# Short blocks from the last to the first, on one side of each matmul of the first phase

## The chip, the cores and the metric

The kernel runs on one core of one Trainium2 chip. The metric is the device time of one execution in microseconds (us); the time of a kernel is the median of several executions. The core has TensorE (PE in the profile; PEld is its loading of weights), VectorE (DVE), ScalarE (ACT), GpSimd (POOL) and SyncE (SP), which issues nearly all of the DMAs.

## The reference

An attention without softmax, normed, feeds a feed-forward block with softplus:

```python
kv  = np.einsum('bhsd,bhse->bhde', k, v)          # (8, 8, 64, 64)
out = np.einsum('bhsd,bhde->bhse', q, kv)         # (8, 8, 576, 64)
rms = np.sqrt(np.mean(out * out, axis=-1, keepdims=True) + 1e-06)
x   = (out / rms * g_norm) -> (4608, 512)
h   = x @ w_in                                    # (4608, 2048)
g   = np.maximum(h, 0.0) + np.log1p(np.exp(-np.abs(h)))
return g @ w_out                                  # (4608, 512)
```

Nearly all of the work is in the last two products.

## The kernel before, in words

**Three factors for each product.** TensorE takes its operands as fp32r. To keep more of the fp32 digits, every operand is split into three pieces (ACT makes the first, DVE the second and third), and every product of two operands is a sum of three matmuls, piece by piece.

**Phases.** The kernel goes through the tokens three times. The *first phase* handles 12 blocks of NT = 384 tokens. In it the attention of the block is computed too (L696 the keys with the values, L720 the rows), the weights are converted and split, and the first chunks of 128 hidden columns are worked off: four chunks each in blocks 0 to 3, six in blocks 4 to 11 (FIRST). That makes 64 steps of one block and one chunk. The later phases (`wide_step`, 48 steps of 512 tokens) take the remaining chunks and add up the partial results.

**A step of the first phase** (`step`) is:

- `mm1` (L864): 12 matmuls of 128x128 weights on a streamed operand of 384 columns, three pieces times four parts of d_model. All 12 accumulate in one PSUM bank `h` (two banks take turns). The weights are pieces of w_in, the streamed operand pieces of x.
- ACT reads `h` and writes the softplus to SBUF as `g` (L886), then makes the first piece `gv[0]` from `g` (L888). DVE makes the second and third piece (L875, L879).
- `mm2` (L871): three times three matmuls. The weights are 128-column parts of `gv`, the streamed operand is a piece of w_out with 512 columns, and the result accumulates over all chunks of the block in one of three banks (`mine`, s0 to s2).
- After the last chunk of a block, `leave` copies each of the three banks to SBUF on ACT (L931) and stores it.

**Order of the work.** The order of the instructions of each engine is made by a planner at build time (`Plan.order`): every task has a cost in ns, a due position and the slots of memory that it takes and gives back, and the planner plays the program through. It has a step's mm2 due one and a half steps after its mm1, so on TensorE mm1 of one step and mm2 of the step before alternate; the small attention matmuls go between them. A change of a task's contents that leaves its cost and slots alone doesn't change the order.

**Traversal of an operand.** `from_the_end(x, w)` cuts the columns of x into blocks of w and goes through the blocks from the last to the first, and through the columns of a block in natural order; w = 0 leaves x as it is. Where the streamed operand and the result of a matmul are both given so, each column of the result stays at its place. Before the change it is used three times: in mm1, for the last of the 12 matmuls alone, with w = 1 on both sides; in `product` (L1066, the first product of the wide steps, 256 columns) with w = 16 and 8 in turn on both sides; and in the wide `mm2` (L1137, 512 columns) with w = 128 on both sides. All other matmuls are in natural order on both sides.

Of the kernel before, what the change touches and what calls it, by code (L numbers as in the profile page):

```python
# [12 lines left out]
AF = mybir.ActivationFunctionType  # L13
# [5 lines left out]
P = 128  # L19
# [4 lines left out]
E = 1.0 / RADIX  # L24
# [17 lines left out]
def from_the_end(x, w):  # L42

    return x.rearrange("p (b w) -> p b w", w=w)[:, ::-1] if w else x


class Slot:
# [13 lines left out]
class Plan:  # L61
# [19 lines left out]
    def slot(self, ring):  # L81
        return Slot(ring)

    def add(self, engine, ns, run, after=(), pos=0.0, take=(), give=(), size=0, behind=None, follows=None, kind="all"):
        pos, behind = round(pos, 4), None if behind is None else round(behind, 4)
        t = Task(engine, ns, run, [a for a in after if a is not None], pos, list(take), list(give), size)
        for s in t.give:
            s.readers += 1
        self.tasks.append(t)
        t.follows = follows  # L90
        t.behind = behind
        t.kind = kind
        return t
# [113 lines left out]
def kernel(  # L207
# [24 lines left out]
    nc = tc.nc  # L232
    B, H, S, D = q.shape
    d_model, d_ff = moe_w_in.shape
# [3 lines left out]
    KD, KF = d_model // P, d_ff // P  # L238
    NT = 384
    TB = NT // P  # L240
# [12 lines left out]
    LAST = 2  # L253
# [32 lines left out]
    scale = const.tile([P, 1], F32, name="scale")  # L286
# [21 lines left out]
    for i in range(3):  # L308
# [10 lines left out]
                 h=2, o=2, tp=1, s0=1, s1=1, s2=1, s3=1, w=15, wh=3, u=4, u1=1, gvp=2, xl=2, ab=2)  # L319
# [9 lines left out]
    slot, add = plan.slot, plan.add  # L329
# [519 lines left out]
    def step(s):  # L849
        n, c = ORDER[s]  # L850
        cs = CHUNKS[n]
        h, g, gv = slot("h"), slot("g"), slot("gv")
        if c == cs[0]:
            sums[:] = [slot(f"s{i}") for i in range(TB)]
        xv, w_in, w_out = xv_slots[n], w_slots[0, c], w_slots[1, c]
        mine = list(sums)
        kept = c >= 4

        def mm1():
            hp = new(h, [P, NT])  # L860
            for m in range(3 * KD):
                i, kd = divmod(m, KD)
                w = 1 if m == 3 * KD - 1 else 0
                nc.tensor.matmul(from_the_end(hp, w), lhsT=w_in.tile[:, i, kd * P:(kd + 1) * P], rhs=from_the_end(xv.tile[:, i, kd], w),  # L864
                                 start=(m == 0), stop=(m == 3 * KD - 1))

        def mm2(i):
            if c == cs[0]:
                new(mine[i], [P, d_model])
            for m in range(3):  # L870
                nc.tensor.matmul(mine[i].tile, lhsT=gv.tile[:, m, i * P:(i + 1) * P], rhs=w_out.tile[:, m],  # L871
                                 start=(c == cs[0] and m == 0), stop=(c == cs[-1] and m == 2))

        def low():
            nc.vector.tensor_tensor(out=gv.tile[:, 1], in0=g.tile, in1=gv.tile.bitcast(F32)[:, 0], op=ALU.subtract)  # L875

        def less():
            f32 = gv.tile.bitcast(F32)
            nc.vector.scalar_tensor_tensor(out=gv.tile[:, 2], in0=f32[:, 1], scalar=-RADIX, in1=f32[:, 0],  # L879
                                           op0=ALU.mult, op1=ALU.add)  # L880

        a = add("PE", 2100, mm1, x_split[n] + factors_done[0, c] + [m for _, m in mm1s[-1:]] +
                (factors_done[1, ORDER[s - 2][1]] if s > 1 else []), s, [h],
                ([xv] if c == cs[-1] else []) + ([w_in] if s == last_step[c] and c != 4 else []))
        mm1s.append((s, a))
        a = add("ACT", 490, lambda: nc.scalar.activation(new(g, [P, NT]), h.tile, func=AF.Softplus, scale=1.0 + E),  # L886
                [a], s, [g], [h])
        a = add("ACT", 530, lambda: nc.scalar.activation(new(gv, [P, 3, NT], F32R)[:, 0], g.tile, func=AF.Copy, scale=DOWN),  # L888
                [a], s, [gv])
        a = add("DVE", 570, low, [a], s, [], [g])  # L890
        a = add("DVE", 570, less, [a], s)
        for i in range(TB):
            a2 = add("PE", 700, lambda i=i: mm2(i), [a] + factors_done[1, c] + [mm2s.get(i)], s + 1.5,
                     [mine[i]] if c == cs[0] else [],
                     [gv] + ([w_out] if s == last_step[c] and not kept else []))
            mm2s[i] = a2
            if c == cs[-1]:
                leave(0, n * TB + i, mine[i], a2, s + 1.5)
# [14 lines left out]
    def leave(ph, t, bank, done, pos):  # L913

        ot = slot("m")
        if ph == LAST and t == n_tiles - 1:
            mid = d_model // 2
            dst = out[t * P:(t + 1) * P]

            def left():  # L920
                nc.scalar.activation(new(ot, [P, d_model])[:, :mid], bank.tile[:, :mid], func=AF.Copy, scale=scale)

            def right():
                nc.vector.tensor_scalar(out=ot.tile[:, mid:], in0=bank.tile[:, mid:], scalar1=scale, scalar2=None, op0=ALU.mult)

            a = add("ACT", 390, left, [done] + scale_done, pos, [ot], [bank])
            b = add("DVE", 430, right, [done] + scale_done, pos + 0.01, [], [bank], follows=a)
            add("SP", 350, lambda: nc.sync.dma_start(out=dst[:, :mid], in_=ot.tile[:, :mid]), [a], pos, [], [ot], 400)
            add("ACT", 100, lambda: nc.scalar.dma_start(out=dst[:, mid:], in_=ot.tile[:, mid:]), [b], pos, [], [ot], 400)
            return  # L930
        a = add("ACT", 690 if ph == LAST else 600, lambda: nc.scalar.activation(  # L931
            new(ot, [P, d_model]), bank.tile, func=AF.Copy, scale=scale if ph == LAST else 1.0),
            [done] + (scale_done if ph == LAST else []), pos, [ot], [bank])
        if ph == LAST and BY_PE <= t < n_tiles - TB:
            n, i = divmod(t, TB)

            def store():
                for m in range(P // BL):
                    a, u = divmod(P // BL * i + m, TB)
                    row = n * NT + u * P + a * BL  # L940
                    nc.sync.dma_start(out=out[row:row + BL], in_=ot.tile[m * BL:(m + 1) * BL])

            add("SP", 1600, store, [a], pos, [], [ot], 750)
            return
        dst = out[t * P:(t + 1) * P] if ph == LAST else dram.tile([P, d_model], F32, name=f"part{ph}_{t}")
        st = add("SP", 350, lambda: nc.sync.dma_start(out=dst, in_=ot.tile), [a], pos, [], [ot], 720)
        part.setdefault(t, []).append((dst, st))
# [96 lines left out]
    def wide_step(k):  # L1044
# [14 lines left out]
        def product(u, q):  # L1059
            f, i = PRODUCTS[u]  # L1060
            w = forms[p][f].tile
            dst, v = unit_slots[ph, n, u]
            for m in range(3):
                for kd in range(2):
                    at = i * 2 * P + kd * P
                    nc.tensor.matmul(from_the_end(place(q), (16, 8)[kd]), lhsT=w[:, m, at:at + P],  # L1066
                                     rhs=from_the_end(dst.tile[:, m, v, kd] if u < 6 else dst.tile[:, m, kd], (16, 8)[kd]),
                                     start=(u == 0 and not m and not kd), stop=(m == 2 and kd == 1), skip_group_check=True)
# [92 lines left out]
        for c in range(2):  # L1161
            for i in range(TW):
                slot_pos = b + PACE + MM2[TW * c + i]
                a2 = add("PE", 700, lambda c=c, i=i: mm2(c, i),
                         [split_done[c]] + factors_done[1, 2 * p + c] + ([seeds[i]] if i in seeds and not c else []) +
                         ([before[i]] if c or not first else []), slot_pos, [mine[i]] if first and not c and ph < LAST else [], [gv] + ([outs[c]] if final else []))
                before[i] = a2
                if last and c:
                    leave(ph, TW * n + i, mine[i], a2, slot_pos)
# [45 lines left out]
    for s in range(len(ORDER)):  # L1215
        step(s)
# [51 lines left out]
```

## Time and profile before

| | |
|---|---|
| three runs | 858.67, 860.09 and 861.0 us; median 860.09 |
| the profiled execution | 858.61 us; span 856.8 us |
| granted TensorE clock | 1.0 of full speed |
| PE, DVE, ACT busy, share of the span | 98%, 82%, 61% |
| L864 (mm1 of the first phase) | 768 matmuls of 384 columns |
| L871 (mm2 of the first phase) | 576 matmuls of 512 columns |
| L1066 and L1137 (wide steps) | 2016 of 256 columns, 1152 of 512 columns |
| L886 softplus, 128x384 | 64, 491 ns each |
| L931 copy of a bank, 128x512 | 72 without scale, 595 ns each |

The first phase takes up the span to about 358 us. Matmuls run in a pipeline: the duration that the profile gives to one (334 to 390 ns) holds its way through the array, and the next one starts before it ends. So the durations of matmuls don't add up to time; the distance from start to start does. In the chain of work that ended last, each piece is given with its start and the time until the next piece takes over, so there the sums over a group of matmuls are that distance times their number.

### The profile page before, as it was taken

Reading aid. Unit: us, or ns where it says so; the run is one execution under the profiler, and the core shown is the slowest. Engines: PE = TensorE matmul, PEld = TensorE weight load, DVE = VectorE, ACT = ScalarE, POOL = GpSimd, SP = SyncE. Lnnn points to the kernel's source line nnn. Section 1 sums busy time; section 2 is a strip of 40 time slices with the busy share of each in tenths; the row PEclk is TensorE's granted clock in tenths of the full one; section 3 lists DMA queues with packets and bytes.
Section 4 is the critical chain, followed back from the end, with each engine's and each line's share of the span. In section 5 each row is a group of like instructions: output and inputs, shape, how many; then the busy total and the mean of one; then the engine's idle time right before and its main releaser. Section 6 shows DMA issues by size and latency. Waiting matters only on the chain.

```text
span 856.8 us, 17075 instructions
## 1 busy us (share of the span) xinstructions
PE 843.8 (98%) x6464; PEld 754.7 (88%) x6464; DVE 704.1 (82%) x995; ACT 520.2 (61%) x980; POOL 76.1 (9%) x79
## 2 busy tenths in 40 slices
PE   7899999999999999999999999999999999999998
PEld 5678898999898999998999999998999899999996
DVE  7988898888788889798898788878788766788873
ACT  6866665446344567776667665655868555566654
POOL 0342224111113300000000000000000000000000
PEclk9999999999999999999999999999999999999999
DMA  9998997778784755436645456645354753777864
GB/s 275 301 228 218 264 270 244 178 243 221 215 186 118 194 159 183 143 112 202 211 156 167 160 160 203 197 158 182 124 195 138 234 167 103 241 242 239 250 189 130
DMA packets 239778, 167.07 MB, mean 195 GB/s; under 512 B 106320, under 2 KB 198736, under 8 KB 239696
## 3 DMA queue, kind: packets, MB, share of 16 engines
q1 hardware_dynamic: 239392, 165.86, 65.8%
q8 instruction: 50, 0.82, 0.4%
q14 instruction: 32, 0.26, 0.1%
q10 hardware_dynamic: 304, 0.13, 0.1%
HBM read 112.98 MB, written 52.95 MB: 194 GB/s over the span
## 4 chain that ended last, share of the span: by engine, by line
PE 94%; DVE 2%; ACT 1%; DMA 1%; issue 1%; POOL 1%; SPq 0%; DVEq 0%; ACTq 0%
PE banks L1137 31%; PE banks L1066 28%; PE banks L871 16%; PE banks L864 15%; PE banks L720 2%; PE banks L696 2%; DMA loads<-in_v_dram 1%; DMA raw<-in_moe_w_in_dram 0%; PE banks L738 0%; POOL roots L728 0%; PE banks L1232 0%; DVE half L732 0%; DVE m L464 0%; DVE m L460 0%; DVE units L643 0%
## 5 line engine op out<-in xcount | busy, mean ns | idle before, releaser
L1137 PE MATMUL banks<-pieces,gv 128*128 128x512 f32 x768 | 236.8, 390 | 0.0
L1137 PE MATMUL banks<-pieces,g_False 128*128 128x512 f32 x384 | 149.4, 389 | 0.0
L1137 PEld LDWEIGHTS banks<-pieces,gv 128*128 128x128 f32 x768 | 132.5, 188 | 17.2 <-DVE banks L910 0.2
L864 PE MATMUL banks<-units,pieces 128*128 128x384 f32 x768 | 145.6, 338 | 0.0
L871 PE MATMUL banks<-pieces,gv 128*128 128x512 f32 x576 | 143.3, 393 | 0.0
L864 PEld LDWEIGHTS banks<-units,pieces 128*128 128x128 f32 x768 | 135.5, 188 | 4.5
L871 PEld LDWEIGHTS banks<-pieces,gv 128*128 128x128 f32 x576 | 106.2, 188 | 19.0
L1066 PEld LDWEIGHTS banks<-units,pieces 128*128 128x128 f32 x840 | 111.0, 188 | 6.5 <-ACT banks L1112 0.4
L1066 PE MATMUL banks<-units,pieces 128*128 128x256 f32 x840 | 115.2, 280 | 0.0
L886 ACT ACTIVATE half<-banks 128x384 f32<-128x384 f32 x64 | 31.4, 491 | 95.7 <-PE banks L864 89.8
L1127 DVE TENSOR_TENSOR gv<-g_True,gv 128x1024 fp32r<-128x1024 f32 x47 | 57.5, 1223 | 36.3 <-ACT gv L1124 36.3
L1137 PEld LDWEIGHTS banks<-pieces,g_False 128*128 128x128 f32 x384 | 72.1, 188 | 15.0
L1066 PEld LDWEIGHTS banks<-units,w 128*128 128x128 f32 x504 | 66.7, 188 | 3.7 <-ACT banks L1112 0.2
L1066 PE MATMUL banks<-units,w 128*128 128x256 f32 x504 | 69.6, 280 | 0.0
L728 POOL TENSOR_TENSOR roots<-roots,half 128x8 f32<-128x8 f32 x36 | 61.9, 1720 | 3.0
L1130 DVE SCALAR_TENSOR_TENSOR g_False<-gv 128x1024 fp32r<-128x1024 f32 x47 | 57.6, 1225 | 1.5
L1029 DVE TENSOR_TENSOR units<-loads,units 128x1024 fp32r<-128x1024 f32 x42 | 51.2, 1219 | 6.0 <-ACT units L1026 5.9
L1094 ACT ACTIVATE g_True<-banks 128x256 f32<-128x256 f32 x96 | 36.7, 384 | 30.6 <-PE banks L1066 29.9
L1116 DVE TENSOR_TENSOR g_True<-banks,g_True 128x512 f32<-128x512 f32 x48 | 33.1, 690 | 25.8 <-PE banks L1066 19.8
L931 ACT ACTIVATE m<-banks 128x512 f32<-128x512 f32 x72 | 42.1, 595 | 17.7 <-PE banks L1137 12.5
L1032 DVE SCALAR_TENSOR_TENSOR units<-units 128x1024 fp32r<-128x1024 f32 x42 | 51.4, 1224 | 1.7
L1026 ACT ACTIVATE units<-loads 128x1024 fp32r<-128x1024 f32 x42 | 44.4, 1056 | 12.7 <-PE banks L1066 10.1
(115 smaller groups left out, 1248.5 us busy)
## 6 DMA issues: line engine op xcount, KB each, us to landing
loads<-x SPq DMA_DIRECT2D x180, 128.0 KB, 2.7
part<-m SPq DMA_DIRECT2D x72, 256.0 KB, 2.9
m<-part SPq DMA_DIRECT2D x72, 256.0 KB, 3.5
loads<-form SPq DMA_DIRECT2D x45, 256.0 KB, 3.2
form<-loads SPq DMA_DIRECT2D x36, 256.0 KB, 3.0
raw<-in_moe_w_in_dram SPq DMA_DIRECT2D x16, 512.0 KB, 4.6
loads<-in_k_dram SPq DMA_DIRECT2D x32, 256.0 KB, 4.5
loads<-in_v_dram SPq DMA_DIRECT2D x32, 256.0 KB, 4.6
```

The costliest lines, as they stand in the source:

```text
L728: nc.gpsimd.tensor_tensor(out=r.tile, in0=r.tile, in1=half, op=ALU.pow)
L864: nc.tensor.matmul(from_the_end(hp, w), lhsT=w_in.tile[:, i, kd * P:(kd + 1) * P], rhs=from_the_end(xv.tile[:, i, kd], w), start=(m == 0), ...
L871: nc.tensor.matmul(mine[i].tile, lhsT=gv.tile[:, m, i * P:(i + 1) * P], rhs=w_out.tile[:, m], start=(c == cs[0] and m == 0), stop=(c == cs ...
L931: a = add("ACT", 690 if ph == LAST else 600, lambda: nc.scalar.activation(new(ot, [P, d_model]), bank.tile, func=AF.Copy, scale=scale if p ...
L1026: nc.scalar.activation(part_of(0, F32R), xl.tile if m > 1 else xl.tile[:, 0], func=AF.Copy, scale=DOWN)
L1029: nc.vector.tensor_tensor(out=part_of(1, F32R), in0=xl.tile if m > 1 else xl.tile[:, 0], in1=part_of(0), op=ALU.subtract)
L1032: nc.vector.scalar_tensor_tensor(out=part_of(2, F32R), in0=part_of(1), scalar=-RADIX, in1=part_of(0), op0=ALU.mult, op1=ALU.add)
L1066: nc.tensor.matmul(from_the_end(place(q), (16, 8)[kd]), lhsT=w[:, m, at:at + P], rhs=from_the_end(dst.tile[:, m, v, kd] if u < 6 else dst. ...
L1094: nc.scalar.activation(dst, src, func=AF.Softplus, scale=1.0 + E)
L1127: nc.vector.tensor_tensor(out=gvt(1, F32R), in0=gt(), in1=gvt(0), op=ALU.subtract)
L1130: nc.vector.scalar_tensor_tensor(out=gt(F32R), in0=gvt(1), scalar=-RADIX, in1=gvt(0), op0=ALU.mult, op1=ALU.add)
L1137: nc.tensor.matmul(from_the_end(mine[i].tile, P), lhsT=(gvt(m, F32R) if m < 2 else gt(F32R))[:, c, i * P:(i + 1) * P], rhs=from_the_end(ou ...
```

## The change

In blocks 1 to 10 of the first phase, one side of every matmul of mm1 is taken in short blocks from the last to the first: either the streamed operand (SHORT[n][0]) or the result (SHORT[n][1]). The other side stays in natural order, so the columns of `h` stand in another order than the tokens; ACT's softplus takes that back, by reading `h` or writing `g` in the same blocks. In mm2 it is the same with LONG: the streamed columns of w_out or the columns of the result. Here the copy in `leave` takes the order back. Block by block, the two products have opposite sides, and the length of the blocks is 16, 16, 1, 1, 8, 8, 4, 4, 32, 32 for blocks 1 to 10. Blocks 0 and 11 are natural throughout, and the reversed last matmul of mm1 is gone in all blocks. The wide steps and the planner's costs are as before.

```diff
+SHORT = [(0, 0), (16, 0), (0, 16), (1, 0), (0, 1), (8, 0), (0, 8), (4, 0), (0, 4), (32, 0), (0, 32), (0, 0)]
+LONG = [(0, 0), (0, 16), (16, 0), (0, 1), (1, 0), (0, 8), (8, 0), (0, 4), (4, 0), (0, 32), (32, 0), (0, 0)]
...
             for m in range(3 * KD):
                 i, kd = divmod(m, KD)
-                w = 1 if m == 3 * KD - 1 else 0
-                nc.tensor.matmul(from_the_end(hp, w), lhsT=w_in.tile[:, i, kd * P:(kd + 1) * P], rhs=from_the_end(xv.tile[:, i, kd], w),
+                nc.tensor.matmul(from_the_end(hp, SHORT[n][1]), lhsT=w_in.tile[:, i, kd * P:(kd + 1) * P],
+                                 rhs=from_the_end(xv.tile[:, i, kd], SHORT[n][0]),
                                  start=(m == 0), stop=(m == 3 * KD - 1))
...
             for m in range(3):
-                nc.tensor.matmul(mine[i].tile, lhsT=gv.tile[:, m, i * P:(i + 1) * P], rhs=w_out.tile[:, m],
+                nc.tensor.matmul(from_the_end(mine[i].tile, LONG[n][1]), lhsT=gv.tile[:, m, i * P:(i + 1) * P],
+                                 rhs=from_the_end(w_out.tile[:, m], LONG[n][0]),
                                  start=(c == cs[0] and m == 0), stop=(c == cs[-1] and m == 2))
...
-        a = add("ACT", 490, lambda: nc.scalar.activation(new(g, [P, NT]), h.tile, func=AF.Softplus, scale=1.0 + E),
+        a = add("ACT", 490, lambda: nc.scalar.activation(from_the_end(new(g, [P, NT]), SHORT[n][0]), from_the_end(h.tile, SHORT[n][1]),
+                                                         func=AF.Softplus, scale=1.0 + E),
                 [a], s, [g], [h])
...
+        r, w = LONG[t // TB] if ph == 0 else (0, 0)
         a = add("ACT", 690 if ph == LAST else 600, lambda: nc.scalar.activation(
-            new(ot, [P, d_model]), bank.tile, func=AF.Copy, scale=scale if ph == LAST else 1.0),
+            from_the_end(new(ot, [P, d_model]), r), from_the_end(bank.tile, w), func=AF.Copy, scale=scale if ph == LAST else 1.0),
             [done] + (scale_done if ph == LAST else []), pos, [ot], [bank])
```

## The prediction

> **What bounds the kernel now.** I read the page's busy times first, then its chain of work that ended last.
>
> ```profile
> PE 843.8 (98%) x6464; PEld 754.7 (88%) x6464; DVE 704.1 (82%) x995; ACT 520.2 (61%) x980; POOL 76.1 (9%) x79
> ...
> PE 94%; DVE 2%; ACT 1%; DMA 1%; issue 1%; POOL 1%; SPq 0%; DVEq 0%; ACTq 0%
> PE banks L1137 31%; PE banks L1066 28%; PE banks L871 16%; PE banks L864 15%; PE banks L720 2%; PE banks L696 2%; DMA loads<-in_v_dram 1%; DMA raw<-in_moe_w_in_dram 0%; PE banks L738 0%; POOL roots L728 0%; PE banks L1232 0%; DVE half L732 0%; DVE m L464 0%; DVE m L460 0%; DVE units L643 0%
> ```
>
> TensorE is the bound: 94% of the chain is PE, and the two lines that the change edits (L864, the first product, and L871, the second) are 31% of it. So what counts is the time from one matmul's start to the next, its pitch. The chain in order of time gives pitches as sums (start us, us, line, matmuls). Here is a stretch of the first phase:
>
> ```profile
> 185.00 0.07 PE banks L696 x3
> 185.06 2.29 PE banks L871 x9
> 187.36 2.08 PE banks L864 x12
> 189.44 2.04 PE banks L871 x9
> 191.49 2.11 PE banks L864 x12
> ```
>
> Three things are to be seen. (a) Settled, a 384-column matmul takes 2.08 / 12 = 173.3 ns and a 512-column one 2.04 / 9 = 226.7 ns. The difference, 53.3 ns for 128 columns, is 0.417 ns a column; so 160.0 + 13.3 and 213.3 + 13.3: each matmul has 13.3 ns on top. (b) A first product that follows a settled second product takes 2.11, not 2.08: by the starts in the trace its first matmuls are 171, 175, 178, 185, 176, 182 ns apart, then 173.3. I call this unsettled; it costs 26 ns. After an unsettled second product the next first product is settled (2.08). (c) A second product after other work is unsettled too (2.29): starts 341, 240, 235, 233, 236, 224, 231, 236, 228 apart; without the first gap, in which its weights are loaded, that is 45 to 50 ns over eight times 226.7. But straight after a first product it is settled (2.04). The last of a first product's twelve matmuls is the only one in this phase with both sides reversed, column by column.
>
> The same view where the two phases meet, and one line from the whole span's chain:
>
> ```profile
> 341.70 0.71 PE banks L1066 x6
> 342.42 2.08 PE banks L864 x12
> 344.50 4.08 PE banks L871 x18
> 348.58 2.11 PE banks L864 x12
> ```
>
> ```profile
> 469.92 2.80 PE banks L1066 x24
> ```
>
> L1066 streams 256 columns with both sides in blocks of 16 and 8 from the end. After it L864 is settled (2.08); after natural L871 it is not (2.11). L1066 after natural order is itself unsettled (0.71 for six against 2.80 / 4 = 0.70). So in these rows what calms a group is the order of the matmul **before** it. And 2.80 / 24 = 116.7 ns is 106.7 for 256 columns by (a) plus 10.0: 3.3 ns less than the 13.3 of natural order.
>
> **The change, part by part.** Blocks 0 to 3 have four steps each and blocks 4 to 11 six. Blocks 1 to 10 change: 54 steps, so 54 x 12 = 648 first-product and 54 x 9 = 486 second-product matmuls. Odd blocks (26 steps) stream the first product's operand in short blocks and write the second's result so; even blocks (28) the other way round. Blocks 0 and 11 lose the reversed last matmul. No instruction, wait or DMA is added or moved, and the planner's costs (490, 600) stay as they are, so the order on every queue is the same. Only durations can change.
>
> *PE, settled pitch.* One reversed side alone is not in the trace. Both sides reversed are: blocks of 128 (L1137) and natural order both give 226.7; single columns cost nothing (a 2.08 group holds one; at double time it would take 2.24); blocks of 16 and 8 go with 3.3 ns less, at 256 columns only. So the ends for a matmul are -3.3 ns and, if it never settles, the mean of the unsettled rows: 177.8 - 173.3 = +4.4 in the first product and 49 / 8 = +6 in the second. I take 0, the row at these widths, where single columns and blocks of 128 gave 0. Ends: -3.3 x 1134 = -3.8 us; +4.4 x 648 + 6 x 486 - 1.2 (unsettled already) = +4.6 us.
>
> *PE, unsettled starts.* Of the 54 first products in blocks 1 to 10, 45 are unsettled now: 45 x 26 ns = 1.2 us. I take it that a reversed side calms the group after it, and that only one of the two sides has this effect; which, I don't know. Either way one parity of blocks keeps today's picture (an effective first product, a natural second one), and in the other it turns round: the first product is calmed (-26 ns), and the second follows an uncalmed first product (+45 ns). About 40 of the 54 second products follow directly; the rest are unsettled already. With 28 steps: 28 x 40/54 x 45 = +0.93, less 28 x 45/54 x 26 = -0.61: +0.3 us (26 steps give the same). Blocks 0 and 11 lose the calming end before some four directly following groups: 4 x 45 = +0.2 us. Ends: -1.8 us if all settle (1.2, and 12 interrupted second products x 50 ns), and +40 x 45 = +1.8 us if nothing calms.
>
> *ACT.* The softplus (54) and the copy out of the bank (30) take the order back, on one side each.
>
> ```profile
> L931 ACT ACTIVATE m<-banks 128x512 f32<-128x512 f32 x72 | 42.1, 595 | 17.7 <-PE banks L1137 12.5 <-PE banks L871 2.6 <-DVE m L464 1.2
> ...
> L886 ACT ACTIVATE half<-banks 128x384 f32<-128x384 f32 x64 | 31.4, 491 | 95.7 <-PE banks L864 89.8 <-DVE w L751 3.1 <-DVE units L643 2.7
> ```
>
> No ACT row reads or writes short blocks. The nearest are a square that reads 128-column blocks (L793, 597 ns, as L931) and, on DVE, a transpose that writes 32-element blocks 96 apart (L819, 707 ns against L751's 687). I take +0 ns, the ACT row; the ends are 0 and double (982 and 1190 ns). What hides it is the wait of PE's order, seen in the timeline:
>
> ```profile
> 174.44 2.20 PE L871 MATMUL banks<-pieces,gv 128*128 128x512 f32 x9
> 174.63 0.49 ACT L886 ACTIVATE half<-banks 128x384 f32<-128x384 f32 x1 [3.10 <-PE banks L864]
> 175.16 0.52 ACT L888 ACTIVATE gv<-half 128x384 fp32r<-128x384 f32 x1
> ...
> 175.71 0.56 DVE L875 TENSOR_TENSOR gv<-half,gv 128x384 fp32r<-128x384 f32 x1 [1.73 <-ACT gv L888]
> ...
> 176.38 0.56 DVE L879 SCALAR_TENSOR_TENSOR gv<-gv 128x384 fp32r<-128x384 f32 x1
> ```
>
> The piece that L879 finishes at 176.94 is first used by the second product at 178.58: 1.64 us of cover, more than the 0.49 of a doubled softplus. This is the usual value; in the changed blocks six steps have under 1 us, and two under 0.5 (steps 7 and 48). The bank that a copy frees is written again 2.4 us after the copy's end at the least in nearly all blocks. Were ACT's price doubled, 54 x 0.49 + 30 x 0.6 = 44 us would be added to an engine that is busy 119 of the 226 us from 110 to 336, and some three uncovered steps would cost 0.5 us each: +1.5 us. DVE reads the softplus's output in natural order as before: 0.
>
> *Sum:* 0 + 0.3 + 0.2 + 0 = **+0.5 us**. The profiled execution took 858.61 us (span 856.8 and 1.8 around it), so 859.1 by it. The median of the three runs is 860.09, 1.5 above: I forecast 860.6.
>
> **The rivals.** *Faster: short blocks take 3.3 ns off whichever side has them, and all groups settle.* -3.8 - 1.1 (most of the 1.8) = -4.9 us: 855.2. For it: L1066's 10.0 against 13.3. Against: the reversed matmuls at 384 and 512 columns show no gain, both of L1066's sides are reversed, and at 397.37 the chain has 24 of the same instructions in 2.95 us, so the 10.0 isn't the pattern's alone. If only the streamed side gains (26 x 12 + 28 x 9 = 564 matmuls), -1.9 + 0.5 = -1.4 us: no change.
>
> *Slower: with one side reversed the pitch never settles.* Every matmul pays the unsettled mean: +4.6 us, 864.7, and with the doubled ACT 866.2. It decides from 2.6 / 1134 = 2.3 ns a matmul. For it: L1066 has stretches at 120 and 121, 122, 116, 118 ns for 18 matmuls on end after a break, so the unsettled state can last. Against: every natural group here is settled after nine matmuls at most, and both patterns are natural on one side.
>
> *Slower: single columns in the result cost the bank's write a second pass.* Those are 72 first-product matmuls (block 4) and 36 second-product ones (block 3): at double streaming time 72 x 160 + 36 x 213 = +19.2 us; with the +0.5, 879.8. Against: the last matmul of every first product writes so, in a 2.08 group. The Trainium skill speaks for it: "PSUM — Partial Sum Buffer", Specifications, says that any non-contiguous pattern slows matmuls significantly. By that rule, the trace doesn't agree: L1066's 116.7 and L1137's 226.7 are written in reversed blocks at no cost.
>
> **How the numbers follow.** No change (within 0.3%, about what a measurement of this kernel can tell) is likeliest: 0.52, with 860.6 and its own range 857.6 to 862.6. Faster 0.16. Slower 0.32: 0.22 for the pitch that doesn't settle, 0.06 for an ACT price above double that uncovers the steps, 0.04 for single columns. The range goes from 855.2 (the first rival) to 866.2 (the second with the ACT price); beyond it lie single columns, most of ACT above double, and a gain larger than L1066's.
>
> **What would show it.** Sums of L864 and L871 in the chain, block by block: 2.08 or 2.11 and 2.04 or 2.09 as forecast; 2.04 and 2.01 in the fast rival; over 2.13 and 2.09 in all blocks in the slow one. Blocks 3 and 4 alone far above 2.2 would be single columns. L886 and L931's means show ACT's price, and idle time of PE before L871 whether it is uncovered. I am wrong at the root if one reversed side does something that neither both nor none did, for which the trace has no row.

## The result and the profile after

| | before | after |
|---|---|---|
| median | 859.53 us (8 runs) | 861.73 us (8 runs) |
| ratio, 95% interval | 1 | 1.0029 [1.0016, 1.0041] |
| the profiled execution, its span | 858.61, 856.8 us | 863.54, 861.7 us |
| start of the first mm1 in the span | 43.75 us | 46.47 us |
| first phase, start of the first mm1 to start of the last mm2 | 313.67 us | 315.86 us |

The ratio is worth 2.5 us (1.4 to 3.5 by its interval); the medians are 2.2 us apart. The two profiled executions are 4.9 us apart: 2.7 of it lies ahead of the first changed instruction (in the profiles below that start wanders between 43.5 and 46.5, whatever the kernel; the granted clock of the first 43 us was 1.00 in the profile before and 0.96 in the one after), 2.2 in the first phase and nothing behind it. So the first phase by the trace, 2.2 us, is the change's price, and it is the measure used below, since it has little noise: in the two kernels below that leave the first phase as it was ("wide_natural" and "wide_sides") it is 313.69 us against 313.67 before.

The page after, its busy times and its chain:

```profile
PE 846.0 (98%) x6464; PEld 755.4 (88%) x6464; DVE 704.2 (82%) x995; ACT 520.3 (60%) x980; POOL 76.4 (9%) x79
...
PE banks L1144 30%; PE banks L1073 27%; PE banks L875 16%; PE banks L867 15%; PE banks L724 2%; PE banks L700 2%; DMA loads<-in_k_dram 1%; PE banks L742 0%; POOL roots L732 0%; PE banks L780 0%; DVE half L736 0%; PE banks L1239 0%; DVE roots L728 0%; DVE units L647 0%; ACT w L806 0%
```

TensorE is the bound as before (L867 is now mm1, L875 mm2, L1073 and L1144 the wide steps), and ACT's time is the same. Here is the chain in order of time (start us, us, line, matmuls): the last mm1 of block 4 (result in single columns) and its last two mm2 (165.47 and 169.68, streamed operand in single columns), then mm1 and mm2 of block 5 (streamed operand of mm1 and result of mm2 in blocks of 8):

```profile
163.38 2.08 PE banks L867 x12
165.47 2.10 PE banks L875 x9
167.57 2.10 PE banks L867 x12
169.68 2.10 PE banks L875 x9
171.78 2.11 PE banks L867 x12
173.88 2.04 PE banks L875 x9
175.93 2.15 PE banks L867 x12
178.08 2.05 PE banks L875 x9
```

Where the result is reversed, the sums are those of natural order: 2.04 to 2.09 for nine and, over all of these groups that follow an mm2 directly, mostly 2.08 to 2.11 for twelve. Where the streamed operand is, mm2 takes 2.10, and by the starts all the way through the group: 233.3 ns a matmul, 20 ns on top of the columns where natural order settles at 13.3. For a streamed mm1 the price isn't one number: in block 5 it takes 2.10 and 2.11 in the first two steps and 2.15 in the others, there with 180 ns from the third matmul on. Two more rows answer to those shown of before, the copy and the softplus on ACT:

```profile
L938 ACT ACTIVATE m<-banks 128x512 f32<-128x512 f32 x72 | 42.1, 595 | 18.6 <-PE banks L1144 12.5 <-PE banks L875 2.7 <-DVE m L468 1.8
...
L891 ACT ACTIVATE half<-banks 128x384 f32<-128x384 f32 x64 | 31.5, 492 | 98.7 <-PE banks L867 95.8 <-DVE units L647 2.9
```

595 and 492 ns against 595 and 491: putting the order back is free on ACT here, in every block (487.8 to 493.3 ns in the mean of each of blocks 1 to 10, single columns included).

Added up over all pairs of neighbouring matmuls of mm1 and mm2 (breaks for other work left out), the time above 173.3 and 226.7 ns a matmul is 1.96 us in the first phase before and 4.13 after, a difference of 2.17 us: the whole of the change's price. By part, against before, with the same groups of the first experiment beside it ("natural", which loses the reversed end of mm1 and has no short blocks):

| groups | after, us | natural, us | short blocks alone |
|---|---|---|---|
| mm2 of even blocks (after: streamed in short blocks) | +1.36 | +0.80 | +0.56 |
| mm1 of odd blocks (after: streamed in short blocks) | +0.61 | +0.03 | +0.58 |
| mm2 of odd blocks (after: result reversed, behind a streamed mm1) | +0.32 | +0.72 | -0.40 |
| mm1 of even blocks (after: result reversed, behind a streamed mm2) | -0.26 | -0.06 | -0.20 |
| blocks 0 and 11 (natural order in both) | +0.14 | +0.11 | +0.03 |

So the price has three parts: the lost reversed end of mm1 (1.6 us of the 2.2, the column "natural"), the groups that stream short blocks (+0.56 and +0.58), and what these give back by calming the group behind them (-0.40 and -0.20).

### The profile page after: what moved, and what is told of

The parts are those of the page before. It is cut to its first block, busy times and chain, and to the rows that moved or that the text cites. A ratio compares the mean times of both kernels' runs of the same rounds, so it can differ in the third digit from the quotient of the medians.

```text
span 861.7 us, 17075 instructions
## 1 busy us (share of the span) xinstructions
PE 846.0 (98%) x6464; PEld 755.4 (88%) x6464; DVE 704.2 (82%) x995; ACT 520.3 (60%) x980; POOL 76.4 (9%) x79
## 4 chain that ended last, share of the span: by engine, by line
PE 94%; DVE 2%; DMA 1%; ACT 1%; POOL 1%; issue 0%; SPq 0%; POOLq 0%; DVEq 0%; ACTq 0%
PE banks L1144 30%; PE banks L1073 27%; PE banks L875 16%; PE banks L867 15%; PE banks L724 2%; PE banks L700 2%; DMA loads<-in_k_dram 1%; PE banks L742 0%; POOL roots L732 0%; PE banks L780 0%; DVE half L736 0%; PE banks L1239 0%; DVE roots L728 0%; DVE units L647 0%; ACT w L806 0%
## 5 line engine op out<-in xcount | busy, mean ns | idle before, releaser
L1144 PE MATMUL banks<-pieces,gv 128*128 128x512 f32 x768 | 236.8, 390 | 0.0
L1144 PE MATMUL banks<-pieces,g_False 128*128 128x512 f32 x384 | 149.4, 389 | 0.0
L1144 PEld LDWEIGHTS banks<-pieces,gv 128*128 128x128 f32 x768 | 132.4, 188 | 17.1 <-DVE banks L916 0.2
L867 PE MATMUL banks<-units,pieces 128*128 128x384 f32 x768 | 145.8, 339 | 0.0
L875 PE MATMUL banks<-pieces,gv 128*128 128x512 f32 x576 | 145.2, 397 | 0.0
L867 PEld LDWEIGHTS banks<-units,pieces 128*128 128x128 f32 x768 | 135.7, 188 | 4.8
L875 PEld LDWEIGHTS banks<-pieces,gv 128*128 128x128 f32 x576 | 106.2, 188 | 20.5
L1073 PEld LDWEIGHTS banks<-units,pieces 128*128 128x128 f32 x840 | 111.0, 188 | 6.4 <-ACT banks L1119 0.4
L1073 PE MATMUL banks<-units,pieces 128*128 128x256 f32 x840 | 115.2, 280 | 0.0
L1144 PEld LDWEIGHTS banks<-pieces,g_False 128*128 128x128 f32 x384 | 72.1, 188 | 15.1
L1073 PEld LDWEIGHTS banks<-units,w 128*128 128x128 f32 x504 | 66.7, 188 | 3.7 <-ACT banks L1119 0.2
L1073 PE MATMUL banks<-units,w 128*128 128x256 f32 x504 | 69.6, 280 | 0.0
L880 DVE TENSOR_TENSOR gv<-half,gv 128x384 fp32r<-128x384 f32 x64 | 35.4, 554 | 21.0 <-ACT gv L894 20.8
```

What stands on the lines that cost most here:

```text
L867: nc.tensor.matmul(from_the_end(hp, SHORT[n][1]), lhsT=w_in.tile[:, i, kd * P:(kd + 1) * P], rhs=from_the_end(xv.tile[:, i, kd], SHORT[n][0]),
L875: nc.tensor.matmul(from_the_end(mine[i].tile, LONG[n][1]), lhsT=gv.tile[:, m, i * P:(i + 1) * P], rhs=from_the_end(w_out.tile[:, m], LONG[ ...
L1144: nc.tensor.matmul(from_the_end(mine[i].tile, P), lhsT=(gvt(m, F32R) if m < 2 else gt(F32R))[:, c, i * P:(i + 1) * P], rhs=from_the_end(ou ...
```

## The experiments

The first four kernels differ from the changed one by the two tables alone (in "both", ACT has nothing to put back). The theory was that the streamed side alone does it; the rivals, that the two sides disagree in their order, or that the lost reversed end of mm1 is the whole price. Three of the later kernels (wide_sides, spread_weights and orders) mix columns and don't put them back, so that their results are others; each was timed once (865.63, 886.69 and 927.22 us), and only their traces are used.

**natural**: every entry of both tables is (0, 0).

> All twelve blocks of the first phase in natural order on both sides, and no reversed last matmul in mm1: the base line for the three kernels beside it. Streamed-side theory (a streamed operand that is taken alone in short blocks from the end keeps its matmuls unsettled; the result's order costs nothing): the calming end of mm1 is lost, so second products that follow directly are unsettled (about 40 x 45 ns = +1.8 us) and the first products after them settled (up to -1.0 us): +0.5 to +0.8 us against before. Transition theory (what costs is the lost calming end, not the short blocks): +2.2 us, as in the changed kernel.

Measured: 1.0028 [1.0016, 1.0039], first phase 315.32 us (+1.65).

```profile
190.86 2.08 PE banks L875 x9
192.95 2.10 PE banks L867 x12
195.05 2.08 PE banks L875 x9
```

Without the reversed end every directly following mm2 is unsettled (2.08, +41 ns), and the mm1 behind it nearly always too (2.10), as it was before the change. I had expected it to be settled there, so the streamed-side theory was wrong on this point, and most of the loss comes from the lost end, as the transition theory had it. By timing, the changed kernel can't be told from this one.

**streamed**: blocks 1 to 10 have (w, 0) in both tables. **result**: (0, w) in both. **both**: (w, w) in both.

```diff
-SHORT = [(0, 0), (16, 0), (0, 16), (1, 0), (0, 1), (8, 0), (0, 8), (4, 0), (0, 4), (32, 0), (0, 32), (0, 0)]
+SHORT = [(w, 0) for w in (0, 16, 16, 1, 1, 8, 8, 4, 4, 32, 32, 0)]    # streamed; LONG the same
```

> Blocks 1 to 10: both products stream in short blocks (16, 16, 1, 1, 8, 8, 4, 4, 32, 32) and both results are natural. Streamed-side theory: second product 486 x 6.6 = +3.2 us, first product 648 x 3.7 = +2.4 less the 1.2 that is there before, so about +4.0 us against before, with sums of about 2.10 for nine and 2.13 for twelve in all ten blocks. Mismatch theory (what costs is that the two sides run in different orders): the same. Transition theory: no more than the natural kernel.

> Blocks 1 to 10: both results are written in short blocks and both streamed operands are natural. Streamed-side theory: as the natural kernel (+0.5 to +0.8 us against before, nine in 2.04 or 2.08, twelve in 2.08 or 2.11). Mismatch theory: as the streamed kernel (+4.0 us). Single columns in the result (blocks 3 and 4) no slower than the others.

> Blocks 1 to 10: streamed operand and result of both products in the same short blocks, so that nothing has to be put back. Streamed-side theory: as the streamed kernel, +4.0 us. Mismatch theory: all groups settled as in the wide steps, -1.5 us against before, or down to -3.8 us more if the 3.3 ns of the wide steps' 256-column matmuls come with it.

| kernel | ratio, 95% interval | first phase, against before |
|---|---|---|
| streamed | 1.0052 [1.0039, 1.0066] | +4.00 us |
| result | 1.0021 [1.0010, 1.0033] | +1.65 us |
| both | 1.0046 [1.0034, 1.0059] | +3.99 us |

Streamed, mm1 and mm2 of block 4 (single columns):

```profile
161.21 2.13 PE banks L867 x12
163.34 2.10 PE banks L875 x9
```

Result, the same stretch as natural above, and then both, in the blocks of 8:

```profile
190.76 2.08 PE banks L875 x9
192.84 2.10 PE banks L867 x12
```

```profile
175.16 2.15 PE banks L867 x12
177.32 2.10 PE banks L875 x9
```

The result's order does nothing: with 1134 matmuls writing in blocks of 32 down to single columns, the first phase takes as long as in natural order (315.32 us in both). What short blocks cost, the streamed operand's order costs: +4.0 us with or without the result turned alike, of which 1.65 is the lost end again and 2.35 the short blocks. The streamed-side theory had worked out +4.0, though its terms as written add up to +4.4. So it is no mismatch of the two sides. In mm2 the length hardly matters from 16 down to 1 (233.2 to 233.7 ns a matmul, against 226.7 settled); 32 costs a little less (232.5 and 232.8). In mm1 twelve take 2.10 to 2.11 with 32, 2.12 with 16 and 2.13 with 4 and 1; with 8 some steps take 2.11 and others of the same block 2.15, which the length can't explain.

**end_of_second** and **end_of_first** vary the calming end.

```diff
+                w = END2[n] if (i, m) == (TB - 1, 2) else 0    # end_of_second: 1, 1, 1, 0, 2, 4, 8, 16, 32, 64, 128, 256
+                w = END1[n] if m == 3 * KD - 1 else 0          # end_of_first: 1, 1, 1, 0, 2, 4, 8, 16, 32, 64, 128, 192; END2 all 1
```

> As before, and the last of a step's nine second-product matmuls has both sides in short blocks too, of another length in each block (1, 1, 1, natural, 2, 4, 8, 16, 32, 64, 128, 256 columns in blocks 0 to 11). End theory (a short-block stream in one matmul calms the group that follows it): the first product that follows directly takes 2.08 instead of 2.11 where the length calms, and the kernel gains up to 1.2 us against before (0.14%); block 3 stays at 2.11. Single columns should calm, as they do at the end of the first product; 128 and 256, nearly natural order, should not. Rival (the second product can't be calmed away, since what follows is 384 columns after 512): 2.11 everywhere, no gain.

> The last second-product matmul of a step in single columns in all blocks, and the last of the first product in blocks of 1, 1, 1, natural, 2, 4, 8, 16, 32, 64, 128, 192 columns. End theory: second products in 2.04 where the length calms and in 2.08 where it doesn't (block 3, and 128 and 192); the first products in 2.08 throughout. Rival: only single columns calm, 2.08 in blocks 3 to 11.

Measured: 1.0001 [0.9991, 1.0011] and 1.0017 [1.0007, 1.0027], first phase +0.20 and +1.09 us. At the end of mm2, single columns don't calm the next mm1 (2.11), against my expectation; 16 and 32 do in part. Block 7, with 16:

```profile
245.19 2.09 PE banks L867 x12
247.28 2.04 PE banks L875 x9
```

At the end of mm1, 2 and 4 calm the next mm2 (2.05, with mm2's own reversed last matmul in it), 8 to 32 in part (2.06 to 2.07), and 64, 128 and 192 not at all (2.08), like natural. The mm1 groups there aren't 2.08 throughout, as I had expected: most take 2.11 or 2.12 in blocks 1 to 8, and mostly 2.08 in blocks 9 to 11, behind an unsettled mm2. So one matmul that streams short blocks shifts something that decides how the next group starts, and which length calms differs between the two products. The end theory holds for mm1's end, and at mm2's end only in part.

**in_turns**: neighbouring matmuls take two lengths in turns, as in the wide steps.

```diff
+TURNS = [(0, 1), (16, 8), (0, 16), (0, 8), (16, 8), (1, 0), (0, 128), (128, 64), (0, 1), (32, 16), (0, 4), (4, 1)]
-                w = 1 if m == 3 * KD - 1 else 0
+                w = TURNS[n][m % 2]                 # mm2: TURNS[n][(3 * i + m) % 2], both sides
```

> Neighbouring matmuls of both products take both sides in two lengths in turns: (0, 1), (16, 8), (0, 16), (0, 8), (16, 8), (1, 0), (0, 128), (128, 64), (0, 1), (32, 16), (0, 4), (4, 1) in blocks 0 to 11, 0 being natural. Theory of change (what settles a matmul is that its neighbour before streams in another order, as at the end of the first product and in the wide steps): settled in most blocks, 2.08 and 2.04 or lower, -1.5 us against before. Streamed-side theory (every matmul that streams short blocks is slower, whatever stands beside it): about half of the loss of the kernel with both sides in short blocks, +2 us.

Measured: 1.0035 [1.0022, 1.0047], first phase +2.54 us. Block 4, with 16 and 8 in turns:

```profile
161.11 2.12 PE banks L867 x12
163.22 2.10 PE banks L875 x9
```

No pair settles: mm2 takes 2.07 to 2.11 in all blocks with a length of 32 or less in them, and 2.08 with (0, 128) and (128, 64). The theory of change falls.

**wide_natural** and **wide_sides** ask why the same order pays in the wide steps.

```diff
-                    nc.tensor.matmul(from_the_end(place(q), (16, 8)[kd]), ...
+                    nc.tensor.matmul(from_the_end(place(q), 0), ...                    # wide_natural, the streamed side too
+                    nc.tensor.matmul(from_the_end(place(q), WIDE_RESULT[n][kd]), ...   # wide_sides; streamed: WIDE_STREAM[n][kd]
```

> First phase as before; the wide steps' first product in natural order on both sides in place of blocks of 16 and 8. If short blocks in turns are what takes 3.3 ns off a 256-column matmul: 120.0 instead of 116.7 ns, 2016 x 3.3 = +6.7 us and unsettled starts on top, some 240 groups x 20 to 40 ns = +5 to +10 us, so +7 to +16 us. If the 10.0 ns belongs to 256 columns and not to the order: +5 to +10 us of unsettled starts alone, or nothing.

> Wide steps, first product, another pair of lengths for its two matmuls in turns in each of the nine blocks of tokens: natural; streamed side alone 16, 8; result side alone 16, 8; both 16, 16; both 8, 8; both 1, 1; both 32, 32; both 128, 64; both 8, 16. In blocks 1 and 2 the columns of the result are mixed, which isn't put back, so those numbers are others. Streamed-side theory: block 1 as before (116.7 ns a matmul), block 2 as natural (119.3). Theory of two sides together: neither of them 116.7. Of lengths: if turns are needed, 16, 16 and 8, 8 are at 119 or above; if short blocks as such do it, 116.7; 128, 64 as natural.

wide_natural: 1.0097 [1.0083, 1.0112], +8.3 us.

```profile
384.65 2.15 PE banks L1066 x18
```

Its 256-column matmuls settle at 120.0 ns (106.7 + 13.3); the first starts behind other groups are shorter (113 to 119 ns), so that the average is 119.3, instead of 116.8 before. And the wide mm2 averages 230.1 instead of 227.1: 2013 x 2.5 + 1150 x 3.0 ns = 8.5 us. So the 10.0 ns on top belong to the order and not to 256 columns as such. wide_sides, block 1 (streamed side alone in 16 and 8), then block 2 (result alone):

```profile
388.06 2.10 PE banks L1070 x18
...
415.20 2.87 PE banks L1070 x24
```

2.10 / 18 = 116.7 ns with the streamed side alone, 2.87 / 24 = 119.6 with the result alone: here too the streamed operand does it, and here it gains. By the mean of all starts, unsettled ones too (starts over 150 ns apart left out, since other waits are in them), the streamed side alone has 117.4 ns in the first wide phase and 118.3 in the second, where before has 117.0 in both in the same block; the result alone has 119.2, 16, 16 has 118.1, single columns 118.3, 8, 16 and 32, 32 have 119.0, 128, 64 119.3, 8, 8 119.6 and natural 119.2. So turns aren't needed for part of the gain, and short blocks as such aren't enough for all of it: both of my readings were too simple.

**spread_weights**: the stationary operand with a step of 4 columns (mm1) or 3 (mm2) in six blocks.

```diff
+                at = slice(kd, None, 4) if SPREAD[n] else slice(kd * P, (kd + 1) * P)      # mm1
+                w, at = STREAM[n], slice(i, None, TB) if SPREAD[n] else slice(i * P, (i + 1) * P)   # mm2
```

> First phase: in some blocks the stationary operand is read with a step of 4 columns (first product) or 3 columns (second) in place of 128 neighbouring ones, so that hidden columns and tokens are mixed and the result is another; the streamed order and the spread are, for blocks 0 to 11: natural, natural + spread, 16, 16 + spread, 1, 1 + spread, 8, 8 + spread, natural + spread, natural, 32 + spread, natural. Theory of two reads (what is on top of the columns, 13.3 ns settled and up to 20, is the weights' read colliding with the stream's, and depends on how the two run against each other): the spread changes the pitch, in blocks 1, 3, 5, 7, 8 and 10 against their neighbours. Theory of the stream alone (the extra time is made where the streamed operand is read, whatever the weights do): no change from the spread, 226.7 natural and 233.3 short.

Block 8, streamed in natural order, mm2 and mm1:

```profile
282.24 2.12 PE banks L877 x9
284.37 2.75 PE banks L869 x12
```

A spread weight load lasts longer by the trace (329 instead of 188 ns in mm1, 254 instead of 188 in mm2). In mm1 it becomes the bound: 233 ns a matmul for 160 ns of columns, with natural, single-column or 32-column stream alike (2.75 / 12 has the first, shorter one in it); with blocks of 16 and 8 it is some 237 and 241. Each of these loads begins 97 ns before the one ahead of it ends, so a load of 254 ns would need 157 for itself, by an estimate from these rows, and fit beside 213 ns of columns in mm2. Yet there the natural stream never settles: 235, 232, 240 ns in turns, 2.12 for nine. So the theory of the stream alone falls for the natural stream. For short blocks the answer is mixed: with spread weights mm2 settles at 233 to 234 in blocks of 16, 1 and 32, about as without, and runs at some 240 in blocks of 8. What is on top of the columns can depend on how the weights are read as well; that the longer load by itself holds mm2 up is unlikely by the estimate, but not excluded.

**orders**: other ways through the streamed operand.

```diff
+ORDERS = [('end', 0), ('inner', 16), ('inner', 4), ('step', 2), ('step', 16), ('end', 64), ('step', 4), ('end', 2), ('inner', 64), ('inner', 2), ('end', 128), ('end', 0)]
+    x = x.rearrange("p (b w) -> p b w", w=w)
+    return x[:, :, ::-1] if how == 'inner' else x.rearrange("p b w -> p w b")
```

> First phase, streamed operand of both products in other orders, result natural, so that the columns are mixed and the result is another: blocks 1 to 10 take blocks of 16 each read backwards in itself; the same with 4; every 2nd column in two passes; every 16th in sixteen passes; blocks of 64 from the end; every 4th column; blocks of 2 from the end; blocks of 64, of 2, each read backwards in itself; blocks of 128 from the end. If going backwards is what costs: the orders with a step forward (2, 16, 4) cost nothing and those backwards in themselves cost as much as short blocks (second product 233 ns). If it is the break every few columns: all but the blocks of 64 and 128 cost. Columns 16 apart far above 233 would be reads that no longer share what one access brings.

Block 1 (16 columns at a time, backwards in themselves), and an mm2 of block 3 (every second column):

```profile
85.62 2.40 PE banks L874 x12
88.02 2.40 PE banks L882 x9
...
129.16 4.08 PE banks L882 x9
```

| streamed order | mm1, mm2 ns a matmul, settled |
|---|---|
| backwards in 2, in 4 columns; blocks of 64, of 128 from the end | 173.3, 226.7 (as natural) |
| blocks of 2 from the end; backwards in 64 columns | 177.8, 233.3 |
| backwards in 16 columns | 200, 266.7 |
| every 2nd, 4th, 16th column | 340, 347, 327 and 453, 461, 434 |

The 226.7 is read where more than nine mm2 matmuls follow one another, which the blocks of 64 and 128 don't have; behind mm1, mm2 takes 2.08 for nine in all four of the free orders, as in "natural". Neither of my two readings holds. Steps forward double the time, so going backwards isn't the price as such; and going backwards within runs of 2 or 4 columns is free, while the runs follow in natural order. Columns 16 apart cost no more than columns 2 apart. The Trainium skill ("SBUF — State Buffer", Door 1, its note on cachelines) says that two hits on a 16-byte line, four fp32 columns, absorb the access, and that each access to a new line pays. The trace fits a unit of four (backwards in 2 and 4 is free, in 16 it isn't; 8 wasn't run) and disagrees on the two hits: every second column has two on each line and takes 453 ns for 213 ns of columns.

**both_ends**: before, and the last matmul of each step's mm2 in blocks of 16 on both sides, the length that calmed an mm1.

> As before, and the last of a step's nine second-product matmuls has both sides in blocks of 16, the length that settled the next first product at the end of the second (2.09 for twelve instead of 2.11, in one block of six steps), while the second product takes 2.05 instead of 2.04 itself. About 18 - 6 = 12 ns for each of some 45 steps: -0.5 us against before in the first phase, less than the timing can show. Rival: the state that the other groups see changes too, and the gain is lost or turns round.

Measured: 0.9992 [0.9981, 1.0003], first phase 313.35 us (-0.3). It can't be told from before by timing; no kernel here is faster than before beyond doubt.

## Why the prediction was right, and where not

The time (861.73) lies in the range and in the likeliest case's own, and no change by the 0.3% bound came true, just (+0.29%, with an interval that reaches 0.41%). That it stayed under the bound is luck: the forecast mechanism is worth +0.5 us and the kernel lost 2.2 to 2.5. The forecast also stood on a median of 860.09 from three runs; eight runs have 859.53, and this alone brings 860.6 half a microsecond nearer to the result.

- *What bounds it* held: all of the price is in the pitch of L867 and L875.
- *Settled pitch* is the term that was mis-sized. I took 0 for either side. For the result that is right (result and natural both 315.32 us). For the streamed operand it is +6.6 ns in mm2 and about +3.7 in mm1 ("streamed"): the unsettled mean that I had set as the upper end (+6 and +4.4), lasting through the group. In the sum this is +1.14 us instead of 0, beyond what natural order costs in the same groups (0.56 and 0.58 in the table). So the slow rival was right for the half of the matmuls that stream short blocks. The rows that I took the 0 from didn't reach so far: a lone single-column matmul at the end of a group is free (2.08), a whole group of them takes 2.13, and blocks of 128 and 64 are free where 32 and shorter are not. My argument against the rival, that one natural side settles, failed: the result's side has no say.
- *Unsettled starts:* that a short-block group calms the next one was right in part, as was that one side alone does it. The streamed side is the one: in "result", mm2 behind a reversed result takes 2.08 as in "natural". Mm1 behind a streamed mm2 gained 0.26 us of the 0.61 forecast, and mm2 behind a streamed mm1 kept 0.32 us where 0 was forecast. The second products behind an uncalmed first product were about as late as forecast (0.80 in "natural" against 0.93); their 1.36 has 0.56 of their own stream on top. Blocks 0 and 11 cost 0.14 (0.2 forecast). Nor does an unsettled second product as a rule settle the next first one, as (b) had read the row at 187.36: natural has 2.10 behind 2.08. And by the starts, 50 of the 54 first products were unsettled before, not 45 (1.3 us, not 1.2).
- *ACT* at 0 was right, single columns too; its cover wasn't needed.
- *Single columns in the result* cost nothing: 2.08 for block 4's mm1 above, and the first phase of "result". The rule that the prediction cites from the Trainium skill ("PSUM — Partial Sum Buffer", Specifications), that any non-contiguous pattern slows matmuls significantly, isn't borne out for these reversed blocks.
- *The sum*, +0.5, is +2.2 in the trace and +2.5 by timing. Of the 1.7 us that it missed, some 1.1 are the settled pitch of streamed groups and the rest is calming that fell short. Seen the other way, the lost end alone is worth 1.65 of the 2.2 (natural), and the short blocks as placed add 0.54 on balance.

What stays open is why. The runs show that the time on top of the columns depends on the order of the streamed read and in some cases on the spread of the weights' read, and not on the result; that the two reads meet in one place of the memory would fit, and is not shown. Nor is it shown why 16 and 8 in turns gain 3.3 ns at 256 columns, and the same pair costs at 384 and 512: besides the width, the operands lie in other places there.

## What to carry to other kernels

Where TensorE is the bound, read the pitch of each group of matmuls from start to start, settled and behind each kind of neighbour: a few ns in a thousand matmuls are a few us. The order of the result in PSUM, and putting it back on ACT, could be had for nothing here; the order of the streamed operand couldn't, and one reversed matmul at a group's end was worth more (1.65 us) than what ten blocks of short ones cost on balance (0.54). Before a term is put at 0 from a row, see that the row holds the same thing: one such matmul in a group isn't a group of them. An order that pays at one width isn't to be carried to another without its own row.

## What was not expected

- A streamed operand read in every second column takes twice as long (453 ns for 512 columns), and one that is read backwards in runs of 16 takes a quarter more: 2.40 us for nine, 266.7 = 213.3 x 1.25 each. Backwards in runs of 4 is free.
- Weights read with a step of 4 columns bound mm1 at 233 ns a matmul or more; with a step of 3, by the estimate above not yet a bound, they still keep a natural-order mm2 unsettled (235 on average).
- Natural order in the wide steps is 8.3 us slower (1.0097) than blocks of 16 and 8 in turns.
